# A fourth K/V buffer, one scaling moved from VectorE to ScalarE, and a regrouped tail in an attention backward kernel

## The chip, the cores and the metric

One core of one Trainium2 chip. The metric is device time in microseconds (us) of one execution; medians over several executions are given with their lowest and highest. PE is TensorE (PEld its weight loads), DVE is VectorE, ACT is ScalarE, POOL is GpSimd, SP is SyncE; SPq and POOLq are the queues from which SP and POOL issue DMAs.

## The reference

Multi-head attention with cached K and V, forward and backward (bf16; B=16, Sq=96, D=640, H=32, Sk=512, Dh=128):

```python
q = (x @ wq).reshape(B, Sq, H, Dh).transpose(0, 2, 1, 3)
scores = jnp.einsum("bhqd,bhkd->bhqk", q, k_cache) * (Dh ** -0.5)
p = softmax(scores)
o = jnp.einsum("bhqk,bhkd->bhqd", p, v_cache)
out = o.transpose(0, 2, 1, 3).reshape(B, Sq, H * Dh) @ wo
_out, _vjp = jax.vjp(f, x, k_cache, v_cache, wq, wo)
return (out, *_vjp(grad_out))          # out, dx, dK, dV, dWq, dWo
```

## The kernel before

An attention loop runs over 16 pairs of heads. A pair begins with a projection (60 matmuls for Q and dO) and then does 32 items, an item being one batch and one head. Its steps are spread over three passes of the loop, so that three items are under way at once; a scheduler then sets the order of instructions on each engine. The parts that the argument touches:

```python
kv = hl.enter_context(tc.tile_pool(name="kv", bufs=3))     # K2h, V2h, KTVT
kvo = hl.enter_context(tc.tile_pool(name="kvo", bufs=2))   # dKVst, the staged dK and dV
psbig = ... tile_pool(name="psbig", bufs=2, PSUM)          # S and dP share two tiles
...
# stage0: load K2h, V2h for batch b+1; 8 PE transposes of K and V -> KTVT (DVE)
# stage1:
bt    = PE transposes of Q and dO
psS   = PE: Q . K^T                  # S,  L170 here (L206 in the changed kernel)
psdP  = PE: dO . V^T                 # dP, L178       (L214)
pe_   = ACT: exp(psS), row sum l_    # exp, L187      (L223)
il    = DVE: 1 / l_
nc.vector.tensor_scalar_mul(out=QdO, in0=bt[:Sq, 0:2*P], scalar1=il)   # QdO, L193 (L229)
junk  = DVE: dP * pe_, row sum dtmp  # L200           (L239)
delta = DVE: dtmp * il
dS    = DVE: (dP - delta) * pe_      # L213           (L252)
# stage2:
bt    = 4 PE transposes of pe_, 4 of dS -> pdT (DVE)       # dS transposes: L275 later
pso   = 8 PE products with V2h, K2h;  odq_st = ACT: pso * il
dkv   = pssm.tile([P, 2, KC, P], F32, name="dkv")          # one PSUM tile, two halves
dkv[:, 1] = 4 PE products of pe_, dO ;  dkv[:, 0] = 4 PE products of dS, Q   # L310 later
nc.scalar.copy(out=dKVst[:, :, hh, :, :], in_=dkv[:])      # ACT, L278 (L317)
if hh == 1: two stores of dKVst from the POOL queue
```

The tail computes gWo and gWq head by head, and then out and dx over 12 blocks of 128 tokens:

```python
gtile, xtile: loads on the SP queue;  WoAll: load on the POOL queue
for h in range(H):
    load Onh, dQnh (POOL queue)
    psw = 24 matmuls, Onh as weights, gtile moving    -> gwo (ACT)   -> store (SP queue)
    psq = 24 matmuls, dQnh as weights, xtile moving   -> gwqt (f32)
    5 f32 PE transposes of gwqt, 5 DVE copies         -> gwq_h       -> store (SP queue)
WqT: transposing load on the SP queue
for t in range(TC):
    OTc, dQTc: transposing loads on the SP queue; 128 matmuls -> out, dx
```

The softmax here doesn't subtract the row's maximum and nothing guards it: scores larger than these inputs give would overflow.

## Time and profile before

2366.57 us is the median of the four runs made first (2362.07 to 2372.9). The figures that carry the argument:

| what | value | from |
|---|---|---|
| busy share of the span, PE / DVE / ACT | 84% / 66% / 49% | the page's first part |
| busy share from 200 to 1500 us, PE / DVE / ACT | 86% / 84% / 64% | busy time by stretch |
| time of the first dS and the last dS | 57.1 and 1829.4 us | the list of instructions on DVE |
| gap at each of the 15 borders between pairs | 17.16 us | distances from dS to dS |
| item time, the mean of the other 496 distances | 3.054 us (median 2.72) | the same |
| tail, from 1832 us to the end of the span | 539 us | span 2371.0 |

The distance from one dS to the next is the measure: there are 512 of them in the loop, they close to the time of the last one, and a change of 0.1 us in the item time is worth 50 us. A mean far above its median, as here, says that some items are stalled and the others are not.

### The profile page before, as it was taken

What the parts mean: (1) busy time and instruction counts of PE and PEld (TensorE: products, weight loads), DVE (VectorE), ACT (ScalarE), POOL (GpSimd) and SP (SyncE); (2) the same over time, 40 slices, a digit from 0 to 9 for tenths busy, and PEclk for the clock granted to TensorE, in tenths of its full rate; (3) what the DMA queues carried; (4) which work ended last, traced back from release to release, by engine and by line L of the source; (5) the groups of instructions that cost most, each with busy time, mean ns of one, the idle gap of its engine ahead of it and who ended that gap; (6) DMA issues with size and microseconds to landing.
All of it is one profiled execution on the core that took longest, in us unless ns stands there. A gap on an engine that the chain in (4) does not pass through costs nothing.

```text
span 2371.0 us, 55735 instructions
## 1 busy us (share of the span) xinstructions
PE 1984.7 (84%) x22624; PEld 1423.7 (60%) x22624; DVE 1571.8 (66%) x4384; ACT 1172.7 (49%) x2201; POOL 477.8 (20%) x641
## 2 busy tenths in 40 slices
PE   3888888888888888888888888888887339999999
PEld 1666666666666766666666666666665215555555
DVE  1977797889798887889787889788878003331000
ACT  1655665666566766666666666566656000000000
POOL 0221222222222222122222222222222102220000
PEclk9998999999999999999999999999999669999999
DMA  8554555555555555455555555555555995554662
GB/s 198 161 162 157 164 173 161 166 166 177 168 171 175 179 175 182 152 178 161 172 169 171 161 175 167 170 161 170 169 161 161 268 174 147 153 151 107 144 144 73
DMA packets 388402, 390.83 MB, mean 165 GB/s; under 512 B 195632, under 2 KB 341040, under 8 KB 387888
## 3 DMA queue, kind: packets, MB, share of 16 engines
q1 hardware_dynamic: 331168, 193.50, 28.9%
q0 software_dynamic: 56976, 193.76, 27.6%
q8 instruction: 177, 2.90, 0.5%
q14 instruction: 81, 0.66, 0.1%
HBM read 173.80 MB, written 173.80 MB: 147 GB/s over the span
## 4 chain that ended last, share of the span: by engine, by line
PE 42%; DMA 28%; DVE 10%; issue 9%; SPq 6%; ACT 5%; POOL 1%; ACTq 0%; POOLq 0%; DVEq 0%
DMA K2h<-in_k_cache_dram 27%; PE big L110 4%; ACT dKVst L278 4%; PE big L100 4%; PE psw L356 4%; PE psw L341 4%; PE dkv L263 4%; SPq L375 3%; PE ktvp L153 3%; PE pso L243 3%; PE pso L251 3%; DVE junk L200 3%; PE big L178 2%; DVE dS L213 2%; PE ktvp L154 2%
## 5 line engine op out<-in xcount | busy, mean ns | idle before, releaser
L278 ACT CAST dKVst<-dkv 128x1024 bf16<-128x1024 f32 x512 | 518.1, 1012 | 179.0 <-PE dkv L271 156.7
L281 POOL DMA_DIRECT2D out_dram<-dKVst x256 | 182.8, 714 | 1435.2 <-ACT dKVst L278 1430.2
L153 PE MATMUL ktvp<-ident,K2h 128*128 128x128 bf16 x2048 | 297.6, 224 | 200.4 <-DMA K2h<-in_k_cache_dram 175.8
L187 ACT ACTIVATE pexp<-big 96x512 bf16<-96x512 f32 x512 | 304.4, 595 | 208.7 <-PE big L170 197.9
L156 DVE TENSOR_SCALAR KTVT<-ktvp 128x1024 bf16<-128x1024 bf16 x512 | 347.5, 679 | 54.3 <-PE ktvp L154 53.5
L200 DVE CUSTOM_DVE_ANT_0 junk<-big,pexp 96x512 bf16<-96x512 f32 x512 | 345.9, 676 | 54.2 <-PE big L178 52.7
L213 DVE SCALAR_TENSOR_TENSOR dS<-big,delta,pexp 96x512 bf16<-96x512 f32 x512 | 377.5, 737 | 0.6
L153 PEld LDWEIGHTS <-K2h 128*128 128x128 bf16 x2048 | 198.5, 99 | 237.3 <-DMA K2h<-in_k_cache_dram 230.5
L258 ACT ACTIVATE odq_st<-pso,il 96x256 bf16<-96x256 f32 x512 | 240.3, 469 | 144.8 <-PE pso L251 127.8
L154 PE MATMUL ktvp<-ident,V2h 128*128 128x128 bf16 x2048 | 293.4, 223 | 0.0
L240 DVE COPY pdT<-bt 128x768 bf16<-128x768 bf16 x512 | 279.9, 547 | 17.8 <-PE bt L236 17.8
L263 PE MATMUL dkv<-QdO,pexp 96*128 96x128 bf16 x2048 | 204.6, 222 | 48.0 <-ACT dKVst L278 35.8
L232 PEld LDWEIGHTS <-pexp 96*128 96x128 bf16 x2048 | 146.4, 99 | 117.7 <-issue 92.7
L154 PEld LDWEIGHTS <-V2h 128*128 128x128 bf16 x2048 | 204.5, 100 | 11.7 <-issue 7.8
L243 PE MATMUL pso<-V2h,pdT 128*96 128x128 bf16 x2048 | 203.6, 222 | 1.2 <-DVE pdT L240 1.2
L251 PE MATMUL pso<-K2h,pdT 128*96 128x128 bf16 x2048 | 203.1, 223 | 0.0
L271 PE MATMUL dkv<-QdO,dS 96*128 96x128 bf16 x2048 | 200.4, 221 | 0.0
L170 PE MATMUL big<-KTVT,QT 128*96 128x512 bf16 x512 | 199.5, 390 | 0.0
L178 PE MATMUL big<-KTVT,dOT 128*96 128x512 bf16 x512 | 198.0, 387 | 1.0
L341 PE MATMUL psw<-gtile,Onh 128*128 128x512 bf16 (+1 forms) x768 | 140.9, 309 | 68.8 <-DMA Onh<-O_scr 40.9
L263 PEld LDWEIGHTS <-pexp 96*128 96x128 bf16 x2048 | 149.2, 99 | 77.2 <-issue 74.6
L236 PEld LDWEIGHTS <-dS 96*128 96x128 bf16 x2048 | 145.1, 98 | 66.2 <-issue 7.8
(53 smaller groups left out, 3267.5 us busy)
## 6 DMA issues: line engine op xcount, KB each, us to landing
out_dram<-dKVst POOLq DMA_DIRECT2D x512, 256.0 KB, 3.3
K2h<-in_k_cache_dram SPq DMA_DIRECT2D x256, 256.0 KB, 3.7
V2h<-in_v_cache_dram SPq DMA_DIRECT2D x256, 256.0 KB, 3.2
O_scr<-odq_st POOLq DMA_DIRECT2D x16, 768.0 KB, 7.4
dQ_scr<-odq_st POOLq DMA_DIRECT2D x16, 768.0 KB, 9.1
Onh<-O_scr POOLq DMA_DIRECT2D x32, 384.0 KB, 5.0
dQnh<-dQ_scr POOLq DMA_DIRECT2D x32, 384.0 KB, 4.3
Wq<-in_wq_dram SPq DMA_DIRECT2D x16, 320.0 KB, 3.4
```

The lines of the kernel that those rows point to most:

```text
L153: nc.tensor.transpose(out=ktvp[:, 0, c, :], in_=K2h[:, hh, c, :], identity=ident[:])
L154: nc.tensor.transpose(out=ktvp[:, 1, c, :], in_=V2h[:, hh, c, :], identity=ident[:])
L156: nc.vector.tensor_scalar_mul(out=KTVT[:], in0=ktvp[:], scalar1=scale)
L178: nc.tensor.matmul(psdP[:Sq, :Sk], lhsT=dOT2[:, hh, t0 : t0 + Sq], rhs=KTVT[:, 1, :, :].rearrange("p c q -> p (c q)"), start=True, stop=True,)
L187: nc.scalar.activation(out=pe_[:], in_=psS[:Sq, :Sk], func=AF.Exp, scale=1.0, accum_out=l_[:])
L200: nc.vector.tensor_tensor_reduce(out=junk[:], in0=psdP[:Sq, :Sk], in1=pe_[:], scale=1.0, scalar=0.0, op0=ALU.mult, op1=ALU.add, accum_out= ...
L213: nc.vector.scalar_tensor_tensor(out=dS[:], in0=psdP[:Sq, :Sk], scalar=delta[:], in1=pe_[:], op0=ALU.subtract, op1=ALU.mult,)
L240: nc.vector.tensor_copy(out=pdT[:], in_=region)
L243: nc.tensor.matmul(pso[:, 0, :], lhsT=pdT[:, 0, c, :], rhs=V2h[:, hh, c, :], start=(c == 0), stop=(c == KC - 1),)
L251: nc.tensor.matmul(pso[:, 1, :], lhsT=pdT[:, 1, c, :], rhs=K2h[:, hh, c, :], start=(c == 0), stop=(c == KC - 1),)
L263: nc.tensor.matmul(dkv[:, 1, c, :], lhsT=pe_[:, c * P : (c + 1) * P], rhs=dOil[:], start=True, stop=True,)
L278: nc.scalar.copy(out=dKVst[:, :, hh, :, :], in_=dkv[:])
```

## The change

Its intent: take the K/V load off the path (one more buffer), unload the busiest vector engine (QdO to ACT), load the tail's first operands during the last pair of heads, and make the tail's products without f32 transposes and with its transposing load out of the way. The diff, cut to its core:

```diff
-        kv = hl.enter_context(tc.tile_pool(name="kv", bufs=3))
+        kv = hl.enter_context(tc.tile_pool(name="kv", bufs=4))
...
-                nc.vector.tensor_scalar_mul(
-                    out=QdO[:], in0=bt[:Sq, 0 : 2 * P]..., scalar1=il[:]
+                nc.scalar.activation(
+                    out=QdO[:], in_=bt[:Sq, 0 : 2 * P]..., func=AF.Copy, scale=il[:],
                 )
...
+            if hp == NHP - 1:
+                # release XT, gT, WoT; gtile, xtile, On4 and dQn4 of two groups in their place
+                add(gtile, gsrc, 4); add(xtile, xsrc, 4)
+                for hg in (0, 4):
+                    add(On4, ..., 6); add(dQn4, ..., 6)      # 14 chunks in all
...
-                    nc.gpsimd.dma_start(out=out_3[...], in_=dKVst[:, 1])
+                    last_st = nc.gpsimd.dma_start(out=out_3[...], in_=dKVst[:, 1])
+                    if hp == NHP - 1 and chunks:
+                        dst_, src_ = chunks.pop(0)
+                        with tc.issue_after(last_st.ins):
+                            nc.gpsimd.dma_start(out=dst_, in_=src_)
...
-        for h in range(H):        # weight gradients head by head, 5 f32 transposes each
+        for hg in range(0, H, HG):                           # groups of four heads
+            # load On4, dQn4 (POOL queue); WoAll after the load of group 3
+            for hh in range(HG):
+                # 24 matmuls of gWo as before; gwo has four buffers
+            for dc in range(DC):
+                # 12 matmuls, weights xtile[:, c, dc], moving dQn4 (512 wide): dWq untransposed
+                # DVE copy to gwq (six buffers), store on the SP queue
...
         WqT = pres.tile([P, H, D], BF16, name="WqT")
-        nc.sync.dma_start_transpose(out=WqT[:], in_=wq)
+        with tc.issue_after(holdW):                          # last gwo store of group 6
+            nc.sync.dma_start_transpose(out=WqT[:], in_=wq)
...
+            with tc.issue_after(hold):                       # last gwq store of group 6
                 nc.sync.dma_start_transpose(out=OTc[:], in_=O2scr[t * P : (t + 1) * P, :])
```

More of the change, by code (lines that the diff above doesn't have):

```diff
@@ L62 @@
     dQ_scr = dram.tile([B, Sq, H, Dh], BF16, name="dQ_scr")
+    O2scr = O_scr.rearrange("b s h d -> (b s) (h d)")
+    dQ2scr = dQ_scr.rearrange("b s h d -> (b s) (h d)")
     with ExitStack() as hl:
-        res = hl.enter_context(tc.tile_pool(name="res", bufs=1))
+        res_cm = tc.tile_pool(name="res", bufs=1, side="right")
+        res = res_cm.__enter__()
+        res_released = False
         XT = res.tile([P, DC, NTOK], BF16, name="XT")
@@ L118, in emit_projection @@
             return QT2, dOT2
+        post_prefetch = {}
         for hp in range(NHP):
@@ L122, with add @@
             QT2, dOT2 = emit_projection(hp)
+            if hp == NHP - 1:
+                res_cm.__exit__(None, None, None)
+                res_released = True
+                presA_cm = tc.tile_pool(name="presA", bufs=1, side="right")
+                presA = presA_cm.__enter__()
+                pwkA_cm = tc.tile_pool(name="pwkA", bufs=2, side="right")
+                pwkA = pwkA_cm.__enter__()
+                gtile = presA.tile([P, TC, D], BF16, name="gtile")
+                xtile = presA.tile([P, TC, D], BF16, name="xtile")
+                post_prefetch["presA_cm"] = presA_cm
+                post_prefetch["pwkA_cm"] = pwkA_cm
+                post_prefetch["gtile"] = gtile
+                post_prefetch["xtile"] = xtile
+                post_prefetch["pwkA"] = pwkA
+                post_prefetch["groups"] = {}
+                chunks = []
+                def add(tile_, src, n):
+                    for c0 in range(0, TC, n):
+                        chunks.append((tile_[:, c0 : c0 + n, :], src[:, c0 : c0 + n, :]))
+                gsrc = g2.rearrange("(p c) d -> p c d", p=P)
+                xsrc = x2.rearrange("(p c) d -> p c d", p=P)
+                add(gtile, gsrc, 4)
+                add(xtile, xsrc, 4)
+                for hg in (0, 4):
+                    On4 = pwkA.tile([P, TC, 4 * P], BF16, name="On4")
+                    add(On4, O2scr[:, hg * P : (hg + 4) * P].rearrange("(p c) d -> p c d", p=P), 6)
+                    dQn4 = pwkA.tile([P, TC, 4 * P], BF16, name="dQn4")
+                    add(dQn4, dQ2scr[:, hg * P : (hg + 4) * P].rearrange("(p c) d -> p c d", p=P), 6)
+                    post_prefetch["groups"][hg] = (On4, dQn4)
             odq_st = st.tile([Sq, 2, B, 2, P], BF16, name="odq_st")
@@ L192, in stage1 @@
                 QdO = wk.tile([Sq, 2, P], BF16, name="QdO")
-                nc.vector.tensor_scalar_mul(
-                    out=QdO[:], in0=bt[:Sq, 0 : 2 * P].rearrange("q (t d) -> q t d", t=2), scalar1=il[:]
+                nc.scalar.activation(
+                    out=QdO[:],
+                    in_=bt[:Sq, 0 : 2 * P].rearrange("q (t d) -> q t d", t=2),
+                    func=AF.Copy,
+                    scale=il[:],
                 )
@@ L284, in stage2 @@
                     )
-                    nc.gpsimd.dma_start(
+                    last_st = nc.gpsimd.dma_start(
                         out=out_3[b, h0 : h0 + 2].rearrange("h (p c) d -> p h c d", p=P),
@@ L306 @@
             )
-    O2scr = O_scr.rearrange("b s h d -> (b s) (h d)")
-    dQ2scr = dQ_scr.rearrange("b s h d -> (b s) (h d)")
+        if not res_released:
+            res_cm.__exit__(None, None, None)
     with ExitStack() as pl:
+        presA_cm = post_prefetch["presA_cm"]
+        pwkA_cm = post_prefetch["pwkA_cm"]
+        gtile = post_prefetch["gtile"]
+        xtile = post_prefetch["xtile"]
+        pwk = post_prefetch["pwkA"]
         pres = pl.enter_context(tc.tile_pool(name="pres", bufs=1))
-        gtile = pres.tile([P, TC, D], BF16, name="gtile")
-        nc.sync.dma_start(out=gtile[:], in_=g2.rearrange("(p c) d -> p c d", p=P))
-        xtile = pres.tile([P, TC, D], BF16, name="xtile")
-        nc.sync.dma_start(out=xtile[:], in_=x2.rearrange("(p c) d -> p c d", p=P))
         WoAll = pres.tile([P, H, D], BF16, name="WoAll")
-        nc.gpsimd.dma_start(out=WoAll[:], in_=wo.rearrange("(h p) f -> p h f", p=P))
-        pwk = pl.enter_context(tc.tile_pool(name="pwk", bufs=2))
+        pwkB = pl.enter_context(tc.tile_pool(name="pwkB", bufs=2))
         psA = pl.enter_context(tc.tile_pool(name="psA", bufs=2, space=bass.MemoryType.PSUM))
@@ L324 @@
         NJ = (D + 511) // 512
-        for h in range(H):
-            Onh = pwk.tile([P, TC, P], BF16, name="Onh")
-            nc.gpsimd.dma_start(
-                out=Onh[:],
-                in_=O2scr[:, h * P : (h + 1) * P].rearrange("(p c) d -> p c d", p=P),
-            )
-            dQnh = pwk.tile([P, TC, P], BF16, name="dQnh")
-            nc.gpsimd.dma_start(
-                out=dQnh[:],
-                in_=dQ2scr[:, h * P : (h + 1) * P].rearrange("(p c) d -> p c d", p=P),
-            )
-            psw = psA.tile([P, NJ * 512], F32, name="psw")
-            for c in range(TC):
-                for j in range(NJ):
-                    w = min(512, D - j * 512)
+        HG = 4 if H % 4 == 0 else 2
@@ new lines @@
+        for hg in range(0, H, HG):
+            if hg in post_prefetch.get("groups", {}):
+                On4, dQn4 = post_prefetch["groups"][hg]
+            else:
+                On4 = pwk.tile([P, TC, HG * P], BF16, name="On4")
+                nc.gpsimd.dma_start(
+                    out=On4[:],
+                    in_=O2scr[:, hg * P : (hg + HG) * P].rearrange("(p c) d -> p c d", p=P),
+                )
+                dQn4 = pwk.tile([P, TC, HG * P], BF16, name="dQn4")
+                last_ld = nc.gpsimd.dma_start(
+                    out=dQn4[:],
+                    in_=dQ2scr[:, hg * P : (hg + HG) * P].rearrange("(p c) d -> p c d", p=P),
+                )
+                if hg // HG == 3:
+                    with tc.issue_after(last_ld.ins):
+                        nc.gpsimd.dma_start(out=WoAll[:], in_=wo.rearrange("(h p) f -> p h f", p=P))
+            for hh in range(HG):
+                h = hg + hh
+                psw = psA.tile([P, NJ * 512], F32, name="psw")
+                for c in range(TC):
+                    for j in range(NJ):
+                        w = min(512, D - j * 512)
+                        nc.tensor.matmul(
+                            psw[:, j * 512 : j * 512 + w],
+                            lhsT=On4[:, c, hh * P : (hh + 1) * P],
+                            rhs=gtile[:, c, j * 512 : j * 512 + w],
+                            start=(c == 0),
+                            stop=(c == TC - 1),
+                        )
+                gwo = pwk.tile([P, D], BF16, name="gwo", bufs=4)
+                nc.scalar.copy(out=gwo[:], in_=psw[:, :D])
+                last_gwo = nc.sync.dma_start(out=out_5[h * P : (h + 1) * P, :], in_=gwo[:])
+            if hg // HG == 6:
+                holdW = last_gwo.ins
+            for dc in range(DC):
+                psq = psA.tile([P, NJ * 512], F32, name="psw")
+                for c in range(TC):
@@ L341 @@
                     nc.tensor.matmul(
-                        psw[:, j * 512 : j * 512 + w],
-                        lhsT=Onh[:, c, :],
-                        rhs=gtile[:, c, j * 512 : j * 512 + w],
+                        psq[:, : HG * P],
+                        lhsT=xtile[:, c, dc * P : (dc + 1) * P],
+                        rhs=dQn4[:, c, :],
                         start=(c == 0),
@@ L347 @@
                     )
-            gwo = pwk.tile([P, D], BF16, name="gwo")
-            nc.scalar.copy(out=gwo[:], in_=psw[:, :D])
-            nc.sync.dma_start(out=out_5[h * P : (h + 1) * P, :], in_=gwo[:])
-            psq = psA.tile([P, NJ * 512], F32, name="psw")
-            for c in range(TC):
-                for j in range(NJ):
-                    w = min(512, D - j * 512)
-                    nc.tensor.matmul(
-                        psq[:, j * 512 : j * 512 + w],
-                        lhsT=dQnh[:, c, :],
-                        rhs=xtile[:, c, j * 512 : j * 512 + w],
-                        start=(c == 0),
-                        stop=(c == TC - 1),
-                    )
@@ L363 @@
-            gwqt = pwk.tile([P, D], F32, name="gwqt")
-            nc.vector.tensor_copy(out=gwqt[:], in_=psq[:, :D])
-            gwq_h = pwk.tile([P, DC, P], BF16, name="gwq_h")
-            for dc in range(DC):
-                pst = psB.tile([P, P], F32, name="pscol")
-                nc.tensor.transpose(
-                    out=pst[:], in_=gwqt[:, dc * P : (dc + 1) * P], identity=identf[:]
-                )
-                nc.vector.tensor_copy(out=gwq_h[:, dc, :], in_=pst[:])
-            nc.sync.dma_start(out=gwq_view[:, :, h * P : (h + 1) * P], in_=gwq_h[:])
+                gwq = pwk.tile([P, HG * P], BF16, name="gwq", bufs=6)
@@ L374 @@
+                nc.vector.tensor_copy(out=gwq[:], in_=psq[:, : HG * P])
+                last_gwq = nc.sync.dma_start(
+                    out=out_4[dc * P : (dc + 1) * P, hg * P : (hg + HG) * P], in_=gwq[:]
+                )
+            if hg // HG == 6:
+                hold = last_gwq.ins
         WqT = pres.tile([P, H, D], BF16, name="WqT")
-        nc.sync.dma_start_transpose(out=WqT[:], in_=wq)
+        with tc.issue_after(holdW):
+            nc.sync.dma_start_transpose(out=WqT[:], in_=wq)
@@ L376 @@
         for t in range(TC):
-            OTc = pwk.tile([P, H, P], BF16, name="OTc")
-            nc.sync.dma_start_transpose(out=OTc[:], in_=O2scr[t * P : (t + 1) * P, :])
-            dQTc = pwk.tile([P, H, P], BF16, name="dQTc")
-            nc.sync.dma_start_transpose(out=dQTc[:], in_=dQ2scr[t * P : (t + 1) * P, :])
+            OTc = pwkB.tile([P, H, P], BF16, name="OTc")
+            with tc.issue_after(hold):
+                nc.sync.dma_start_transpose(out=OTc[:], in_=O2scr[t * P : (t + 1) * P, :])
@@ L381 @@
+            dQTc = pwkB.tile([P, H, P], BF16, name="dQTc")
+            with tc.issue_after(hold):
+                nc.sync.dma_start_transpose(out=dQTc[:], in_=dQ2scr[t * P : (t + 1) * P, :])
             pso = psA.tile([P, NJ * 512], F32, name="psw")
@@ L391 @@
                     )
-            ot = pwk.tile([P, D], BF16, name="ot")
+            ot = pwkB.tile([P, D], BF16, name="ot")
             nc.scalar.copy(out=ot[:], in_=pso[:, :D])
@@ L406 @@
                     )
-            gxt = pwk.tile([P, D], BF16, name="gxt")
+            gxt = pwkB.tile([P, D], BF16, name="gxt")
             nc.scalar.copy(out=gxt[:], in_=psg[:, :D])
             nc.gpsimd.dma_start(out=gx2[t * P : (t + 1) * P, :], in_=gxt[:])
+        pwkA_cm.__exit__(None, None, None)
+        presA_cm.__exit__(None, None, None)
 _INS = ['x', 'k_cache', 'v_cache', 'wq', 'wo', 'grad_out']
```

## The prediction

> **What bounds the kernel now.** I read the table of busy time by stretch first, to split the program, then the list of instructions in time on VectorE, then the waits and the chain, because the shares of the whole span mix two programs: an attention loop (16 pairs of heads of 32 items each, one item being one batch and head) and a tail of two matrix products (the weight gradients, then the output and the input gradient). Columns: stretch in us, its length, busy us of each engine with its instruction count, granted TensorE clock, DMA share, GB/s.
>
> ```profile
> 40.00:1832.00 1792.00, 1530.04 (x19390) 1167.99 (x19388) 1498.79 (x4192) 1132.30 (x2144) 393.60 (x540) 0.98 0.54 167
> 1832.00:1945.00 113.00, 35.54 (x219) 18.84 (x219) 7.67 (x19) 3.11 (x5) 17.27 (x17) 0.67 1.07 218
> 1945.00:2155.00 210.00, 207.03 (x1463) 117.27 (x1464) 63.05 (x167) 19.38 (x28) 52.84 (x52) 0.98 0.56 150
> 2155.00:2371.00 216.00, 210.93 (x1552) 119.15 (x1549) 2.28 (x6) 16.61 (x24) 13.02 (x24) 1.00 0.50 118
> ```
>
> The loop is 1792 us with PE at 85% and DVE at 84%: neither is saturated on average. The first 113 us of the tail are nearly lost for PE (35.5 busy), with DMA saturated (1.07). After that PE is full.
>
> Inside the loop, one item on DVE:
>
> ```profile
> 1005.10 0.69 DVE L200 CUSTOM_DVE_ANT_0 junk<-big,pexp 96x512 bf16<-96x512 f32 x1 [0.28 <-PE big L178]
> 1005.71 0.08 DVE L200 DVE_READ_ACCUMULATOR2_ANT dtmp<- 96x1 f32 x1
> 1005.71 0.34 DVE L193 TENSOR_SCALAR QdO<-bt,il 96x256 bf16<-96x256 bf16 x1
> 1005.98 0.14 DVE L211 TENSOR_TENSOR delta<-dtmp,il 96x1 f32<-96x1 f32 x1
> 1006.04 0.54 DVE L240 COPY pdT<-bt 128x768 bf16<-128x768 bf16 x1
> 1006.51 0.73 DVE L213 SCALAR_TENSOR_TENSOR dS<-big,delta,pexp 96x512 bf16<-96x512 f32 x1
> 1007.17 0.67 DVE L156 TENSOR_SCALAR KTVT<-ktvp 128x1024 bf16<-128x1024 bf16 x1
> 1007.77 0.15 DVE L191 RECIPROCAL il<-l 96x1 f32<-96x1 f32 x1
> 1007.84 0.66 DVE L200 CUSTOM_DVE_ANT_0 junk<-big,pexp 96x512 bf16<-96x512 f32 x1
> ```
>
> Read the starts, not the durations: neighbours overlap by some 80 ns. From junk to junk are 2.74 us without a gap, so here DVE is the bound. Over the whole trace, the distance from one dS to the next has a median of 2.72 us. By halves of a batch: second head 2.75 us on average, first head 3.33 us, up to 7. The first head of each batch is the one that needs a freshly loaded K and V. The tile view of K2h says what it waits for; the chain of waits agrees:
>
> ```profile
>   DMA K2h<-in_k_cache_dram: 406.2, 337
> ...
> DMA to landing us min/median/max: 2.8/3.7/6.2
> ```
> ```profile
> DMA K2h<-in_k_cache_dram 27%; PE big L110 4%; ACT dKVst L278 4%; PE big L100 4%; PE psw L356 4%; PE psw L341 4%; PE dkv L263 4%; SPq L375 3%; PE ktvp L153 3%; PE pso L243 3%; PE pso L251 3%; DVE junk L200 3%; PE big L178 2%; DVE dS L213 2%; PE ktvp L154 2%
> ```
>
> (The 406 counts the weight load and the matmul of the same wait.) One K2h load is issued at 1004.97 and its tile is wanted before 1008.57, 3.6 us later, which is one median landing: the load cannot be issued earlier because its buffer is still being read by pso. So the loop alternates between a DVE bound and a buffer-bound DMA latency. The sum closes: 57 us to the first dS, 15 boundaries between head pairs of 17.1 us (the projection, 60 matmuls), and 496 distances with a mean of (1829.4 - 57.1 - 257)/496 = 3.055 us.
>
> For the tail, in time order, the chain has:
>
> ```profile
> 1834.52 8.60 DMA dQ_scr<-odq_st
> 1844.06 78.39 SPq L375
> 1923.27 5.15 SPq L378
> ```
>
> The transposing load of WqT holds the sync queue for 78 us, and the stores of gwo and gwq stand behind it, so the two output buffers fill and PE stops; before that PE waits 40.9 us for the first Onh.
>
> **What the skill says.** "ScalarE: Activation LUTs", section What ACT_TABLE_LOAD costs, gives 186 ns + 0.833 ns an element, 93 ns more for each pointer operand, and back-to-back overlap of 93 ns. For QdO (256 elements, scale from a pointer) that is 492 ns; the trace's own odq_st, the same shape from f32, takes 469, so about 0.47 us, some 0.38 net. "Perfetto Trace Analysis", Optimization Strategy, says that a bubble that repeats on an engine that should be saturated can mean too few buffers; the 3.33/2.75 alternation is such a bubble. "DMA: Bandwidth & Descriptors", Queues, rings and completion order, says that each DMA engine shares itself round-robin by packet between queues. The trace fits: WqT's 256-byte packets took 19 ns where WoT was loaded alone at the start, and 28 to 62 ns beside the 4096-byte packets of Onh and dQnh. The same page, Latency and other measured facts, gives 261 GB/s for a DMA transpose; WoT's 5.24 MB moved at 262.
>
> **The change, part by part.**
>
> *A fourth kv buffer.* The load for a batch can be issued one batch earlier, so the lead grows from 3.6 us to about 3.6 + 2 items = 9 us, above the longest landing (6.2). The K2h wait should nearly vanish. Alone it would take the mean from 3.055 to about 2.76 (DVE bound 2.72 and a little jitter): 496 x 0.30 = 146 us.
>
> *QdO to ACT.* DVE loses the 0.27 us between the starts of QdO and delta: its bound falls to 2.45. ACT per item, by starts: dKVst 0.91, exp 0.49, accumulator read 0.30, odq 0.38, QdO 0.38 = 2.46. PE needs about 2.2. Three engines are now level, so I look at a loop across engines in the built order (PE: dP, four transposes, dS transposes, dkv, three transposes, next S ...; ACT: exp, odq, QdO, dKVst; DVE: il, junk, pdT, delta, KTVT, dS). From the end of dS(n-1): dS transposes and dkv on PE until dKVst(n-1) starts 0.69; dKVst to exp(n+1) 0.91; exp to dP(n+1) 0.65; dP to junk(n+1) 0.42; then DVE to the end of dS(n+1): 0.60 + 0.47 + 0.07 + 0.60 + 0.74 = 2.46. That is 5.13 us for two items, 2.57 each, above the DVE bound. With jitter I take 2.62. So the loop saves 496 x (3.055 - 2.62) = 216 us, some 70 of it from QdO.
>
> *Prefetch in the last head pair.* gtile, xtile and the first two groups of O and dQ (10.2 MB) are loaded in 14 chunks behind the stores. A batch already moves 1.05 MB in about 5.2 us with DMA near 62% (0.54 x 1792/1574); another 0.66 to 0.79 MB pushes it to about full. I charge 8 us. It removes the 41 us wait at the start of the tail.
>
> *Weight gradients.* The old form makes dWq transposed and turns it back with 160 f32 transposes (53.0 us of PE by their group) and 160 copies. The new form has xtile as the weights, so these go. PE per group of four heads: 4 x 3.26 (24 matmuls of gWo, start to start) + 60 x 0.216 = 26.0; eight groups 208 us.
>
> *WqT moved* behind group 6, WoAll behind group 3. No large load then runs beside WqT: 5.24 MB at 262 GB/s is 20 us, plus latency. It starts about 173 us into the tail and frees the queue near 197; the five gwq stores and the first OTc (5 us issue, 7.4 landing) follow, done near 208, just when PE ends group 7. Gap 0 to 5 us.
>
> *Last phase* unchanged: 12 x 17.38 = 208.6, and 5 us to the end.
>
> Tail: 208 + 4 + 208.6 + 5 = 426, against 2371 - 1832 = 539: 113 saved. Loop end: 57 + 15 x 17.1 + 496 x 2.62 + 8 + 3 = 1624. Sum 2050 us.
>
> **Rivals.** (1) *QdO on ACT gives nothing back*: it stands ahead of dKVst in ACT's order and itself waits for il from DVE, so ACT may set a loop of 2.75 or more; for it, ACT at 2.46 has only 4% to spare against 2.57; against, dkv ends later than QdO would in my loop. Then +65 us: 2115. (2) *DMA takes K2h's place*: the stores have two dKVst buffers and must land in about 6.8 us (three items less dKVst), against a landing of 3.3 median and 6.5 at most after 1.4 us of issue. An occasional stall, 10 to 30 us in all. (3) *WqT still takes 78 us at its new place*: then OTc comes 50 us late and PE idles: 2100. Against it: that load was queued behind gtile and xtile and shared with WoAll. (4) *All goes to the DVE bound*, 2.47: 1976; the loop of 2.57 speaks against it.
>
> **Range and chances.** The certain parts (fewer f32 transposes, prefetch, K2h wait) are worth over 200 us, so a change within 2% (47 us) needs two rivals at once and a new stall besides. The uncertain term is the item time: 0.1 us is 50 us. 2.55 without other losses gives 2010, 2.72 with a small gap gives 2105. Predicted 2050, range 2005 to 2110; faster 0.97, within 2% 0.02, slower 0.01.
>
> **What would show it.** A distance from dS to dS near 2.6 with no alternation between first and second head; the K2h wait under 60 us; ACT busy near 86% in the loop; PE starting the tail within 3 us of the loop's end; WqT's issue near 22 us rather than 78; under 6 us of PE gap before the last phase. It would be wrong if dP or junk now waits for exp in each item, if ACT waits for il before QdO with DVE idle too, if DMA stays full in the last head pair for more than 20 us extra, or if SP blocks gwq's stores.

## The result, and the profile after

| kernel | median us | lowest to highest | runs |
|---|---|---|---|
| before | 2367.17 | 2354.36 to 2384.98 | 16 |
| changed | 2068.05 | 2066.82 to 2069.98 | 11 |

The ratio is 0.8734, interval 0.8715 to 0.8753: faster. The predicted 2050 us was 18 us too low, within the range.

Busy time by stretch of the changed kernel (stretch, length, busy us of PE, PEld, DVE, ACT and POOL with counts, granted clock, DMA share, GB/s): the loop, the weight gradients, the last phase.

```profile
40.00:1646.00 1606.00, 1540.76 (x19395) 1173.61 (x19394) 1381.53 (x3680) 1299.30 (x2656) 403.09 (x555) 1.00 0.59 192
1646.00:1855.00 209.00, 209.00 (x1259) 106.59 (x1258) 27.66 (x40) 22.14 (x32) 16.84 (x17) 1.00 0.69 209
1855.00:2067.00 212.00, 206.87 (x1524) 116.87 (x1522) 0.00 (x0) 16.61 (x24) 13.01 (x24) 1.00 0.56 131
```

The loop lost 186 us (1792 to 1606) and the tail 118 (539 to 421). The granted clock in the loop went from 0.98 to 1.00, and with it a K transpose from 224 to 219 ns by its group on the page; no run separates this from the stalls that went. PE is full from the tail's first microsecond; the stretch in which it did 35.5 us of work in 113 is gone.

The tile view of K2h in the changed kernel gives the time for which an engine sat idle until a K load had landed (us, times):

```profile
  DMA K2h<-in_k_cache_dram: 1.7, 2
```

It was 406.2. The time from the issue of a K2h load to its first use has grown from a median of 4.1 to 8.0 us.

The tail on PE, in time order (start, length, line, operation), first and last of the weight-gradient groups and the start of the last phase:

```profile
1645.15 13.20 PE L392 MATMUL psw<-gtile,On 128*128 128x512 bf16 x96
...
1840.12 13.11 PE L407 MATMUL psw<-dQn,xtile 128*128 128x512 bf16 x60
1853.07 8.86 PE L437 MATMUL psw<-WoAll,OTc 128*128 128x512 bf16 x64
```

The last phase starts where the last group ends: no gap. The queue behind it, in the changed kernel, shows the WqT load holding the sync queue for 20 us where it had held it for 78:

```profile
1815.78 19.89 SPq L425 DMA_TRANSPOSE WqT<-in_wq_dram  x1
1835.77 3.46 SPq L416 DMA_DIRECT2D out_dram<-gwq  x5
1840.45 4.92 SPq L429 DMA_TRANSPOSE OTc<-O_scr  x1
```

The waits of the kernel before, between 1832 and 1945 us, say what those 78 us had cost (engine, line, what it waited for: us in total, times, longest):

```profile
ACT gwo L349 <- DMA out_dram<-gwo: 37.9, 1, 37.9
DVE gwq_h L371 <- DMA out_dram<-gwq_h: 32.2, 1, 32.2
PE psw L341 <- DMA Onh<-O_scr: 40.9, 1, 40.9
PE psw L341 <- ACT gwo L349: 27.9, 1, 27.9
```

The PE lines are the loss: 40.9 us for the first Onh and 27.9 for ACT, which itself stood at a gwo store behind WqT. The tail's gain splits so. The kernel before needs 7.41 us a head (the distance of gwo copies when nothing is stalled), 237 us for 32 heads, with 208.6 for the last phase and 5 to the end: 451 of 539, so 88 us were stalls. The changed kernel takes 26.0 us a group, 208 for eight: 29 us less for the products. 88 + 29 = 117.

The loop is where the time is not what was predicted. With no stalls left, the item takes 2.684 us on average (median 2.68), not 2.62. Here is one item of the changed kernel, in time order, cut to the instructions that bind it:

```profile
900.90 0.60 ACT L223 ACTIVATE pexp<-big 96x512 bf16<-96x512 f32 x1
...
901.64 0.38 PE L214 MATMUL big<-KTVT,dOT 128*96 128x512 bf16 x1
...
902.08 0.34 PE L275 MATMUL bt<-ident,dS 96*128 96x96 bf16 x4
...
902.25 0.39 PE L310 MATMUL dkv<-QdO,dS 96*128 96x128 bf16 x4
...
902.72 1.01 ACT L317 CAST dKVst<-dkv 128x1024 bf16<-128x1024 f32 x1 [0.21 <-PE dkv L310]
```

The exp of the next item starts at 903.62. From exp to exp: dP starts 0.74 us after exp (it waits for exp to have read its PSUM tile); the dS transposes, of the item before, 0.44 after dP, because four K/V transposes stand between them in PE's order; the dkv products 0.17 later; dKVst 0.47 later, when the last of them is done (ACT waits 0.21 for it); and the next exp stands behind dKVst on ACT, 0.90 later. The sum is 2.72. In every other item the fourth step is 0.42 or so and the sum is 2.68. So one item goes round between ACT and PE and back, and neither is at its limit: from 200 to 1500 us ACT is busy 81%, PE 96%, DVE 86% (run 4 below gives PE and DVE the same work in a shorter item). DVE does not set the pace: it waits for dP 194 times in that stretch, 33.1 us in all.

### The profile page after: what moved, and what is told of

It reads as the page before. It is cut to its first block, busy times and chain, and to the rows that moved or that the text cites. A ratio compares the mean times of both kernels' runs of the same rounds, so it can differ in the third digit from the quotient of the medians.

```text
span 2067.1 us, 54551 instructions
## 1 busy us (share of the span) xinstructions
PE 1958.7 (95%) x22176; PEld 1397.8 (68%) x22176; DVE 1409.2 (68%) x3720; ACT 1339.3 (65%) x2713; POOL 434.0 (21%) x603
## 4 chain that ended last, share of the span: by engine, by line
PE 53%; DVE 17%; issue 16%; ACT 10%; SPq 2%; DMA 1%; POOL 1%; ACTq 0%; POOLq 0%; DVEq 0%
DVE junk L239 9%; PE big L214 9%; ACT pexp L223 7%; DVE pdT L279 6%; PE pso L282 6%; PE big L104 5%; PE big L114 5%; PE psw L392 5%; PE psw L407 5%; ACT dKVst L317 3%; PE pso L290 3%; PE dkv L302 3%; PE dkv L310 3%; PE ktvp L189 2%; PE bt L275 2%
## 5 line engine op out<-in xcount | busy, mean ns | idle before, releaser
L189 PE MATMUL ktvp<-ident,K2h 128*128 128x128 bf16 x2048 | 386.1, 219 | 6.7 <-DVE KTVT L192 3.8
L190 PE MATMUL ktvp<-ident,V2h 128*128 128x128 bf16 x2048 | 336.7, 219 | 0.0
L229 ACT ACTIVATE QdO<-bt,il 96x256 bf16<-96x256 bf16 x512 | 240.3, 469 | 44.5 <-DVE il L227 15.0
L282 PE MATMUL pso<-V2h,pdT 128*96 128x128 bf16 x2048 | 216.8, 228 | 41.6 <-DVE pdT L279 4.2
L190 PEld LDWEIGHTS <-V2h 128*128 128x128 bf16 x2048 | 197.6, 96 | 71.7 <-issue 17.0
L282 PEld LDWEIGHTS <-pdT 128*96 128x96 bf16 x2048 | 141.1, 122 | 123.0 <-DVE pdT L279 123.0
L302 PE MATMUL dkv<-QdO,pexp 96*128 96x128 bf16 x2048 | 198.7, 219 | 0.2
L206 PE MATMUL big<-KTVT,QT 128*96 128x512 bf16 x512 | 193.9, 379 | 0.0
L121 DVE CAST dOT<-big 128x512 bf16<-128x512 f32 x96 | 66.5, 693 | 183.7 <-PE big L114 183.7
L271 PEld LDWEIGHTS <-pexp 96*128 96x128 bf16 x2048 | 144.4, 97 | 60.6 <-issue 0.3
```

The source lines that it names most:

```text
L189: nc.tensor.transpose(out=ktvp[:, 0, c, :], in_=K2h[:, hh, c, :], identity=ident[:])
L190: nc.tensor.transpose(out=ktvp[:, 1, c, :], in_=V2h[:, hh, c, :], identity=ident[:])
L282: nc.tensor.matmul(pso[:, 0, :], lhsT=pdT[:, 0, c, :], rhs=V2h[:, hh, c, :], start=(c == 0), stop=(c == KC - 1),)
L302: nc.tensor.matmul(dkv[:, 1, c, :], lhsT=pe_[:, c * P : (c + 1) * P], rhs=dOil[:], start=True, stop=True,)
```

## The experiments

**The first theory**, after the result: (a) the fourth buffer alone removes the stalls; (b) the item is then bound by this loop of one item between ACT and PE, so QdO's move is worth only the distance from the DVE bound of 2.72 to 2.684; (c) the tail adds its 117 us whatever the loop does. The rivals: that the move to ACT, rather than the buffer, freed the loop; that DVE or ACT alone bounds the item; that prefetch and tail changes paid for each other. Each run stood beside seven runs of the kernel before on the same chip: medians 2382.39 (first four runs below), 2380.16 (7, 8, 6 and 9) and 2382.12 (5, 10 and 11). The kernel before varies by over 1% (2363 to 2391 in the fast runs of the first of these); the changed forms without stalls repeat within 0.4%, so I compare those by their medians and by their traces. The changed kernel itself was not run again beside them: its 2068.05 is from the runs of the result, and a difference from it of a few us is safe only where the traces show it too.

| run | edit | median us | ratio to before | item time us |
|---|---|---|---|---|
| 1 | changed, three kv buffers | 2210.62 | 0.9279 | 2.985 |
| 2 | changed, QdO on DVE | 2084.27 | 0.8757 | 2.714 |
| 3 | before, four buffers and QdO on ACT | 2184.61 | 0.9178 | 2.681 |
| 4 | changed, dkv in two PSUM tiles | 1989.04 | 0.8349 | 2.511 |
| 5 | before, four buffers | 2196.64 | 0.9215 | 2.713 |
| 6 | changed, WqT not held back | 2102.75 | 0.8840 | 2.681 |
| 7 | run 4 with QdO on DVE | 2121.93 | 0.8924 | 2.784 |
| 8 | run 4 with three dKVst buffers | 1981.30 | 0.8325 | 2.494 |
| 9 | changed, prefetch not spaced | 2080.74 | 0.8746 | 2.710 |
| 10 | run 6, third group's loads behind WqT | 2068.78 | 0.8678 | 2.684 |
| 11 | run 8, ten chunks prefetched | 1980.28 | 0.8313 | 2.490 |

**Run 1: three buffers again, all else changed.**

```diff
-        kv = hl.enter_context(tc.tile_pool(name="kv", bufs=4))
+        kv = hl.enter_context(tc.tile_pool(name="kv", bufs=3))
```

> Changed kernel with kv back at three buffers, all else kept. Buffer theory: in the changed kernel a K2h load has 8.0 us from issue to first use (median over the 256 loads; 4.1 in the kernel before, where it is late). One buffer less takes two items off, 8.0 - 5.4 = 2.6 us, less than the median landing of 3.7, so the first head of each batch waits again by 1 us or more: alternation of first and second head, K2h wait back to over 150 us, time about 2250 (2170 to 2360). Rival (the fourth buffer is idle capacity, the gain came from QdO and the order of instructions): within 1% of the changed kernel, 2068.

Measured: 2210.62 us (2194.77 to 2218.99), less than expected but in its range. Waits of this run between 200 and 1500 us:

```profile
PEld L189 <- DMA K2h<-in_k_cache_dram: 144.1, 165, 2.9
```

The wait for K is back. So the buffer, not the new place of QdO, had removed it.

**Run 2: QdO back on VectorE, all else changed.**

```diff
-                nc.scalar.activation(out=QdO[:], in_=..., func=AF.Copy, scale=il[:])
+                nc.vector.tensor_scalar_mul(out=QdO[:], in0=..., scalar1=il[:])
```

> Changed kernel with QdO back on VectorE. The scheduler then gives the old order on PE, DVE and ACT. Theory: the item is bound by DVE again, 2.72 to 2.76 us from dS to dS against 2.68 measured with QdO on ACT, so the move is worth only 20 to 40 us: 2090 to 2108. The prediction on record had put 70 us on it: 2138. Rival (ACT is now so full that QdO there costs as much as it frees): same time or faster, up to 2060.

Measured: 2084.27 us (2083.48 to 2085.87), 16 us over the changed kernel and under the expected range. The last dS comes at 1657.4 instead of 1642.8 us; the item is at 2.714, the DVE bound. QdO's move, for which the prediction had some 70 us, was worth 15 to 16.

**Run 3: the kernel before with both changes to the loop and its old tail.**

```diff
-        kv = ...bufs=3            |  nc.vector.tensor_scalar_mul(out=QdO[:], ...)
+        kv = ...bufs=4            |  nc.scalar.activation(out=QdO[:], ..., scale=il[:])
```

> Kernel before with only the two changes of the loop: four kv buffers and QdO on ACT; the tail is the old one. Theory (loop and tail add up): loop as in the changed kernel, dS to dS 2.68, tail as before 539 us against 421, so 2068 + 118 = 2186. Rival (the two help each other, the prefetch or the new tail speeds or slows the loop): off by over 20 us.

Measured: 2184.61 us (2181.42 to 2188.78). Last dS at 1641.0, as in the changed kernel; the rest, 2184.6 - 2068.1 = 117 us, is the tail. Loop and tail add up.

**Run 4: dkv as two PSUM tiles.** This is the test of the loop. The dV half needs no dS; copied by itself, it can be done before dS arrives, and only half of the copy is left on the path.

```diff
-                dkv = pssm.tile([P, 2, KC, P], F32, name="dkv")
+                dkvV = pssm.tile([P, KC, P], F32, name="dkvV")
...              # four products of pe_ and dO into dkvV
+                nc.scalar.copy(out=dKVst[:, 1, hh, :, :], in_=dkvV[:])
+                dkvK = pssm.tile([P, KC, P], F32, name="dkvK")
...              # four products of dS and Q into dkvK
-                nc.scalar.copy(out=dKVst[:, :, hh, :, :], in_=dkv[:])
+                nc.scalar.copy(out=dKVst[:, 0, hh, :, :], in_=dkvK[:])
```

> Changed kernel with dkv as two PSUM tiles, each copied out by ACT on its own (dV once its products are done, dK after). Theory: the item of the changed kernel is set by a loop of ACT and PE: exp to dP 0.74, dP to the transposes of dS 0.44, to the products of dkv 0.17, to dKVst 0.45, dKVst to the next exp 0.91 = 2.71. The copy that stands in the loop is halved (0.91 to 0.50), but the built order puts eight transposes instead of four before dS's: 0.74 + 0.66 + 0.17 + 0.45 + 0.50 = 2.52. DVE's own bound is 2.45. So 2.50 to 2.58 an item, 496 x 0.13 = 65 us less: about 2003. Rivals: DVE or DMA sets the item: no change (2068); ACT is the bound by its busy time: slower, as one more instruction adds about 0.09 us an item, 2110.

Measured: 1989.04 us (1984.42 to 1990.81), 79 us faster than the changed kernel although ACT has one instruction more in each item. The items have a median of 2.47 us. On DVE in run 4:

```profile
835.21 0.67 DVE L239 CUSTOM_DVE_ANT_0 junk<-big,pexp 96x512 bf16<-96x512 f32 x1
...
835.82 0.56 DVE L279 COPY pdT<-bt 128x768 bf16<-128x768 bf16 x1
...
836.36 0.68 DVE L192 TENSOR_SCALAR KTVT<-ktvp 128x1024 bf16<-128x1024 bf16 x1
836.96 0.74 DVE L252 SCALAR_TENSOR_TENSOR dS<-big,delta,pexp 96x512 bf16<-96x512 f32 x1
...
837.68 0.68 DVE L239 CUSTOM_DVE_ANT_0 junk<-big,pexp 96x512 bf16<-96x512 f32 x1
```

From junk to junk are 2.47 us, each start where its predecessor's work ends: DVE has no slack left here, at about the 2.45 that the prediction had worked out for it. But the loop of ACT and PE closes at the same length: exp to dP 0.74, to the dS transposes 0.66 (eight transposes stand between now), to the dkvK products 0.17, to the copy 0.42, to the next exp 0.48 (medians of this trace), 2.47 in sum. So both bounds have met, and this trace does not say which of them holds the item. That the gain came from a second PSUM tile alone, and not from the shorter copy, does not fit the changed kernel: there PE stood idle before the products of pe_ for 0.1 us in 1300. The rival that ACT alone bounds the item is out: with more work on ACT the item is shorter. In the last pair of heads there is a new wait:

```profile
ACT dKVst L309 <- DMA out_dram<-dKVst: 15.4, 9, 4.2
```

That pair takes 96.3 us where the others take 76.3.

**Run 5: the fourth buffer alone.**

```diff
-        kv = hl.enter_context(tc.tile_pool(name="kv", bufs=3))     # in the kernel before
+        kv = hl.enter_context(tc.tile_pool(name="kv", bufs=4))
```

> Kernel before with four kv buffers and nothing else: the old order of instructions, QdO on VectorE, the old tail. Theory (loop and tail add up): its loop is that of the run with QdO back on VectorE (2084), its tail that of the kernel before, 117 us longer as the run of the loop alone showed (2185 against 2068): 2201, and 2.72 from dS to dS without alternation. The prediction on record gave the buffer alone 146 us: 2221.

Measured: 2196.64 us (2196.47 to 2196.76). The item falls from 3.054 to 2.713 and the last dS from 1829.4 to 1657.8: 172 us in the traces, 185 between the medians of these rounds. The prediction had 146 for it. The runs now lie within 0.3 us of each other: their spread went with the stalls.

**Run 6: WqT not held back.** The scheduler then issues it after the second gwo store of the first group.

```diff
-        with tc.issue_after(holdW):
-            nc.sync.dma_start_transpose(out=WqT[:], in_=wq)
+        nc.sync.dma_start_transpose(out=WqT[:], in_=wq)
```

> Changed kernel with the WqT load no longer held back to the seventh group; the built order puts its issue after the second store of gwo of the first group. The prefetched gtile and xtile are no longer ahead of it, so it should hold the sync queue for 20 to 45 us and not 78, beside the loads of the third group. With four gwo and six gwq buffers PE can run some 32 us before it stops. Theory (most of the old stall came from what was queued before and beside WqT): 0 to 12 us more, 2068 to 2080. Rival (the place of WqT is what matters): 30 us more or over, 2100.

Measured: 2102.75 us, in two values, 2090 and 2114: a miss for my theory. The rival had the number; run 10 shows that its reason, the place of WqT, is not the cause. The sync queue and PE in the profile of a 2114 run:

```profile
1657.14 66.33 SPq L424 DMA_TRANSPOSE WqT<-in_wq_dram  x1
```
```profile
1726.80 1.87 PE L407 MATMUL psw<-dQn,xtile 128*128 128x512 bf16 x4 [43.46 <-ACT gwo L400]
```

The stores of gwo stand behind the load again and PE idles 43 us. Busy time by stretch while WqT is loading, in run 6 first and then in the changed kernel, says why it takes long; read the last two columns:

```profile
1671.00:1683.00 12.00, 11.95 (x90) 6.80 (x89) 0.03 (x1) 1.38 (x2) 0.62 (x1) 1.00 1.25 70
```
```profile
1818.00:1836.00 18.00, 18.00 (x109) 9.13 (x108) 2.77 (x4) 1.38 (x2) 0.00 (x0) 1.00 1.23 267
```

The DMA share is the same, and 70 GB/s move instead of 267. In those stretches a 256-byte packet of the transpose took 170 ns on average in run 6, beside the 4096-byte packets of On4 and dQn4, and 19 ns alone. These 12 us are not the whole load: in stretches of 6 us the rate goes up and down between 44 and 262 GB/s. From 1685 to 1722 us, where PE stands idle, it is 149 GB/s and a packet takes 52 ns on average; over the whole load it is 47 ns, with a median of 18: a part of the packets is held up long, most are not.

**Run 7: run 4 with QdO back on VectorE.** It completes the square of split and QdO.

```diff
-                nc.scalar.activation(out=QdO[:], in_=..., func=AF.Copy, scale=il[:])
+                nc.vector.tensor_scalar_mul(out=QdO[:], in0=..., scalar1=il[:])
```

> The split copy of dkv, with QdO back on VectorE; completes a square with the changed kernel (2068, dS to dS 2.68), QdO on DVE (2084, 2.72) and the split (1989, 2.47). Theory (two bounds lie close together: DVE with QdO 2.72, the loop of ACT and PE 2.68; each hides the other): the split is worth nothing while QdO is on DVE, 2.72 to 2.74 an item, 2080 to 2095. So the move of QdO is worth about 0.25 us an item, 100 us or more in all, once the loop is gone, and 16 without. Rival (the split itself shortens the item by its new order of instructions, wherever QdO is): below 2040.

Measured: 2121.93 us (2119.98 to 2125.87), a miss: I had expected the split to help, or to do nothing, here too, and it costs 38 us. Items of 2.81 us (median), above the DVE bound of 2.72. One item of run 7:

```profile
919.65 0.59 ACT L223 ACTIVATE pexp<-big 96x512 bf16<-96x512 f32 x1
...
920.39 0.38 PE L214 MATMUL big<-KTVT,dOT 128*96 128x512 bf16 x1 [0.43 <-ACT pexp L223]
...
920.60 0.38 PE L279 MATMUL pso<-V2h,pdT 128*96 128x128 bf16 x4
...
921.16 0.34 PE L272 MATMUL bt<-ident,dS 96*128 96x96 bf16 x4
921.33 0.39 PE L309 MATMUL dkvK<-QdO,dS 96*128 96x128 bf16 x4
...
921.76 0.58 ACT L316 CAST dKVst<-dkvK 128x512 bf16<-128x512 f32 x1
...
922.47 0.59 ACT L223 ACTIVATE pexp<-big 96x512 bf16<-96x512 f32 x1
```

It is the same loop with other lengths. The scheduler has put eight pso products and two transposes, not four transposes, between dP and the dS transposes: that step is 0.77 us instead of 0.44. The exp then waits not for ACT but for S, 0.71 after the copy began. The sum is 2.82. So an edit that moves no work at all onto PE changed PE's order, and by this trace the order set the time. The worth of QdO's move follows: with three buffers 37 us by the last dS of before and run 1 (1829.4 and 1792.9), or 55 by the medians of their rounds less 117 for the tail, in forms that vary by more than the difference; 16 with four, and 133 with four and the split (runs 4 and 7). No single figure belongs to it.

**Run 8: a third buffer for dKVst, on run 4.**

```diff
-        kvo = hl.enter_context(tc.tile_pool(name="kvo", bufs=2))
+        kvo = hl.enter_context(tc.tile_pool(name="kvo", bufs=3))
```

> The split with three dKVst buffers instead of two. In the split's last head pair dS to dS goes up to 9.0 us and the pair takes 96.3 us against 76.3 for the others; ACT waits 15.4 us there for stores of dKVst, which stand behind the prefetch chunks. Theory: one more buffer hides most of it, 10 to 20 us less: 1969 to 1979. Rival (DMA is simply full there): no change, 1989.

Measured: 1981.30 us (1974.56 to 1982.19), 8 us less where 10 to 20 were expected: a small miss. The last pair goes from 96.3 to 91.7 us, not to 76, which is about half of the gain; the other half is 0.26 us in each of the other 15 pairs (76.60 to 76.34 on average), as from 60 to 1460 us ACT had waited 3.9 us for stores in run 4 and no longer does. The wait for stores there is replaced in part by one for K2h, 13 us. This pair moves the prefetch as well as its own traffic.

**Run 9: the prefetch issued in program order at the tail** instead of one chunk behind each batch's stores.

```diff
-                    if hp == NHP - 1 and chunks:
+                    if False:
...
+        for k_, (dst_, src_) in enumerate(chunks):      # in the tail
+            (nc.sync if k_ < 6 else nc.gpsimd).dma_start(out=dst_, in_=src_)
```

> Changed kernel with the 14 prefetch chunks issued at the start of the tail instead of in the last head pair. Theory: PE then waits for gtile and the first On before its first product, about 12 to 18 us (a chunk lands in 6 to 7 us, two queues share the engines), and the last head pair gets no faster, as it costs nothing there now (83.5 us against 83.2): 2080 to 2086. Rival (prefetch was worth the whole 41 us wait of the kernel before): 2109.

Measured: 2080.74 us (2078.87 to 2081.90). The number was as expected, but not for the expected reason. The scheduler moved these loads up into the last pair, in one bunch; PE starts the tail at once, as in the changed kernel. The loss is in the last pair (96.1 us instead of 83.5), where one wait does most of it:

```profile
ACT dKVst L317 <- DMA out_dram<-dKVst: 9.0, 1, 9.0
```

So this run shows that spacing the chunks out is worth 13 us, or that and the queue together: the edit also put the first six chunks on the sync queue. What the prefetch as a whole is worth in the tail it does not show; that the kernel before lost 40.9 us there is all that speaks for it.

**Run 10: run 6, with the O and dQ loads of the third group on the sync queue behind WqT.**

```diff
+                ldq = nc.sync if hg // HG == 2 else nc.gpsimd
-                nc.gpsimd.dma_start(out=On4[:], ...)
+                ldq.dma_start(out=On4[:], ...)
...              # the same for dQn4
```

> The early WqT of the run before (2103, WqT's issue 66 us, PE idle 43.5 us), with On and dQn of the third group issued on the sync queue behind WqT instead of on the GpSimd queue beside it. Theory (it is not WqT's early place but the transfers of O and dQ in a second queue that slow it: 27 to 30 GB/s of transpose beside them, 266 alone): WqT issue back to 20 to 25 us, no PE idle, 2065 to 2080. Rival (the early place itself, or the strided writes of gwo and gwq): WqT over 40 us again and 2090 or more.

Measured: 2068.78 us (2067.92 to 2069.41), the time of the changed kernel. WqT's issue takes 19.87 us at the same early place. So it is the loads that another queue moves beside the transpose that make it slow, not its place in the program.

**Run 11: run 8 with only the first group prefetched**, ten chunks instead of 14.

```diff
-                for hg in (0, 4):
+                for hg in (0,):
```

> The split with three dKVst buffers (1981), with only the first group of O and dQ prefetched: 10 chunks, the second group loaded at the start of the tail, where it is wanted 26 us later. Theory (DMA is full in the last head pair, 91.7 us against 76.3): 3.1 MB less there, 5 to 9 us saved, 1972 to 1976. Rival (the pair suffers from the first chunks as much as from the last, or the tail now waits): 1981 or more.

Measured: 1980.28 us (1980.10 to 1985.92): no change against run 8's 1981.30, where 5 to 9 us less were expected: a miss. The last pair is at 89.8 us, still 13 over the others, so the number of chunks is not what makes it long, or not these four. Nor is DMA full over the whole pair, as the theory had it: its share from 1465 to 1556 us is 0.81 here and 0.80 in run 8. This stays open.

Runs 8 and 11 beat both kernels: 1980 against 2367 and 2068.

## Why the prediction was right or wrong

The mechanism was right for the buffer and the tail, and the total near; the loop that was to bind the item afterwards was not the one that binds it. The total is in part near by luck: the term for QdO was 55 us too good, and three others were 36 us too bad. By its own steps:

- **A fourth kv buffer.** Right, and larger than said: run 5 takes the item to 2.713 (predicted 2.76), 496 x (3.054 - 2.713) = 169 us, not 146. The K2h wait fell to 1.7 us, where under 60 was asked. The estimate of a lead of 9 us was close to the 8.0 measured.
- **QdO to ACT.** This is the step that failed. Predicted: a loop of two items through DVE, "5.13 us for two items, 2.57 each", with jitter 2.62, and some 70 us. Measured: 2.684, 496 x (2.713 - 2.684) = 14 us. The prediction's loop left dS, reached dKVst 0.69 us later, and came back to dS through exp, dP and junk. It took PE to be free when dS was done. In the trace it is not: dS ends at 901.87, and its transposes start at 902.08, since dP and four K/V transposes stand ahead of them in PE's order, and dP waits for exp. With that edge, a shorter loop of one item closes, exp to dP to dS transposes to dkv to dKVst to exp, 2.68 to 2.72 us. Its step from exp to dP is 0.74, where the prediction had 0.65: in 97% of the items from 200 to 1500 us dP starts 0.14 us after exp has ended. The prediction had the order ("PE: dP, four transposes, dS transposes, dkv"), and followed only the data. The term for the accumulator read, 0.30 us on ACT, was wrong as well (0.09 from start to start where nothing waits), without effect on the time; so was a sum (its DVE steps add up to 2.48, not 2.46, which makes the loop 2.575).
- **The loop together.** 496 x (3.054 - 2.684) = 184 us against 216: 32 us short, the buffer 23 better and QdO 55 worse.
- **Prefetch in the last pair.** 8 us were charged, none were paid: the last pair takes 83.5 us, pair 9 takes 83.2. That is 8 us better. With a loop at 2.47 the same pair does cost (runs 4 and 8), so the charge belongs to a faster loop than this one.
- **Weight gradients.** 26.0 us a group, 208 in all: right.
- **WqT.** Issue 19.89 us for about 22, no gap before the last phase: right. Rival 3, that it still takes long, fell for this kernel, but runs 6 and 10 show what it hung on: no second queue loading beside it.
- **Tail.** From 1646 us to the end are 421 us, predicted 426.
- **Rivals.** Of rival 1 the first half held: the move gave almost nothing, by a loop through ACT and not by ACT's own sum. Rival 2, the stores, appears in the last pair, in forms that are faster or load it more (runs 4, 8 and 9); before it, from 60 to 1460 us, ACT waits for them 0.9 us in the changed kernel and 3.9 in run 4. Rival 4, the DVE bound, was ruled out by a loop in the prediction; it was kept out by another, and run 4 reached 2.47.

The errors sum: 2050 + 32 - 8 - 5 = 2069, against 2067 of the profile. Of the signs that the prediction named, the alternation of first and second head is nearly gone (distances of 3.34 and 2.75 on average became 2.64 and 2.73) and PE starts the tail at once, as it said; ACT's busy share is 81% rather than 86, as fits an item longer than 2.62. One sign that it named for being wrong did appear: dP waits for exp in each item.

What is shown and what is argued: that the copy of dkv was in the binding loop is shown by run 4, and that neither DVE nor PE alone was the bound follows from it, as their work is the same there. That PE's order makes the loop's length is read from the traces of the changed kernel and of run 7; no run changes the order alone, because the scheduler sets it and every edit moved something with it.

## What to carry to other kernels

When stalls are removed and no engine is full, look for a loop across engines that includes the order in which each engine stands, not only the data that it passes; list start to start until it closes on itself, and cut the longest copy in it so that only the half that depends on the late operand stays. An operation's worth when it is moved depends on what bounds the loop at that time (16, some 37 to 55, or 133 us here for the same move), and an edit can change the order on an engine that it does not touch, so compare the built orders before counting on a gain. A transposing load wants its time without large loads on a second queue: 20 us alone and 66 beside them here.

## What the Trainium skill lacked or had wrong

- "DMA: Bandwidth & Descriptors" names the sharing by packet between queues ("Queues, rings and completion order"), and a rate of 261 GB/s for a transpose ("Latency and other measured facts"; 267 GB/s here alone: agrees). It lacks the case of a transpose beside large loads of another queue: in one stretch of 12 us the whole traffic fell to 70 GB/s at the same DMA share (1.25 and 1.23) and a 256-byte packet took 170 ns on average instead of 19; in the 37 us in which PE was idle it was 149 GB/s and 52 ns; and the issue held its queue for 66 us instead of 20. Taking turns by packet says why the small packets get a small share, not why the sum falls.
- "Perfetto Trace Analysis" says that repeating bubbles can mean too few buffers ("Optimization Strategy"); run 5 agrees (172 us by its traces for one buffer). It gives no way to find what comes next, a loop across two engines that takes in the order on each, where neither is at its limit (ACT at 81%, PE at 96%, 2.684 us an item, and 2.47 once its copy is split).
- "ScalarE: Activation LUTs" ("What ACT_TABLE_LOAD costs") fits QdO (estimate 492 ns from its figures; 469 measured, and 0.36 to 0.40 us from start to start where nothing waits). It gives no cost for the accumulator read that follows an exp with a row sum: 197 ns, but only 0.09 us from start to start.
- No page that I used says that moving one operation can let the scheduler change the order on a third engine: in run 7 this made an item 2.81 us where run 4 has 2.47.
